# Scores of all pairs in row groups, one tile for the mixing sequences, and two-tensor work on VectorE

## The chip, the cores and the metric

The kernel runs on one core of a Trainium2 chip. The metric is the time of one execution on the device in microseconds (us); lower is better. Engines are named as the profile names them: PE is the matrix engine TensorE (PEld its weight load), DVE is VectorE, ACT is ScalarE, POOL is GpSimd, SP issues most transfers.

## The reference

The reference is a gated linear attention whose output goes through a Fourier mixing layer and a feed-forward network. There are 4 batches, 8 heads, 768 tokens, 48 values a head, so a model width of 384; the hidden width is 1536. All is float32.

```python
for t in range(S):                       # attention, per batch and head
    state = alpha[:, :, t, :, None] * state + einsum('bhd,bhe->bhde', k[:, :, t], v[:, :, t])
    y[:, :, t] = einsum('bhd,bhde->bhe', q[:, :, t], state)
x = y.transpose(0, 2, 1, 3).reshape(B, S, H * D)
X = np.fft.fft(np.fft.fft(x, axis=1), axis=2)      # mixing
u = x + np.real(X)
un = (u - mean(u)) / sqrt(var(u) + 1e-6)           # over the model width
out = u + maximum(un @ w_ch1, 0.0) @ w_ch2
```

## The kernel before, in words

**Pairs.** Two heads make a pair, four pairs a batch, sixteen in all. A pair lies with one head on partitions 0 to 47 and the other on 64 to 111, time along the row. `attn_stages` lists a pair's stages. In `s1` DVE scans alpha forward and backward over 768 steps (tiles `w`, from `w3()`, and `al`), resets at every chunk of 64 and scales every second chunk (`first`). `s2` and `s3` multiply the scanned products into k and q (`times`, tile `kq`). `s4` transposes k (`kt`). `s5` or `s5r` makes the scores of each 128-token block, in two halves of three blocks; ACT moves them out of PSUM and POOL masks them with `affine_select`. `s6` makes the states at block bounds: PE products, then a chain of five DVE operations in `tt`. `s7` multiplies scores and states with v and q; ACT writes the result to two `y` tiles a batch.

**Scores in two forms.** `s5` multiplies the heads apart in plain float32, 64 and 48 partitions deep: the heads lie on different row groups of PE's array. `s5r`, for pairs from number `FR = 7` on, splits q and k into a high and a low part in a faster format (tile `qs`; two ACT activations, one ACT cast and three DVE operations a half) and does both heads in one set of nine matmuls 256 wide a half.

**Mixing.** `combine` takes a pair's columns of the two `y` tiles and forms sum and difference (`sd`, 288 elements a row) and six sequences (`z`, 96 elements each: six two-tensor operations and two with a scalar). The six sequences of a batch lie in three `w3` tiles (`w6`). When the batch is whole, `f2` folds them four ways for the Fourier transform along the width, tile by tile; `mk_s` and `mk_d` are the transforms on PE. Half the tokens come back through memory in reversed order, gathered by POOL's transfers (`f0`). Then `norm_stages` and `ffn_stages`: split operands `x` and `h`, 864 matmuls of 384 columns each way for the run, DVE's `h<-f,h` standing between the two layers.

**Weights.** `wsplit` unpacks twelve tiles of 64-bit words into high and low parts, with three integer operations on DVE, `wm` and `wd` (768 elements, two tensors each) and ACT work. Six are written ahead of the first FFN part, six within it.

**What sets the order.** All operations are recorded first (`Engine.__getattr__`, line 464; nearly every row of the profile has this line). `Plan.emit` then places them one at a time: the engine whose next operation can start earliest, and on it the lowest key among those ready within `WINDOW`. `duration` prices each operation, `LAT` each hop between engines. `FX` names the engines that may do a kind of operation, 'G' being POOL and 'V' DVE; where it names two, the operation goes to one unless the other would be done earlier by `SLACK`. `port` and `held` model that DVE and POOL hinder each other: an overlap lengthens both by half of it. Up to a modelled time of `WARM = 120` us, gaps of PE are filled with small matmuls on `zero` (line 1146). So a changed price or rule reorders all engines.

```python
FX = {'comb': 'G', 'mul': 'VG', 'first': 'G', 'wm': 'VG', 'wd': 'VG', ...}
SLACK = {'ACT': 2.0, 'DVE': 0.5, 'POOL': 5.0}
return [s1, s2, s3, s4, s5 if pair < FR else s5r, s6, s7, lambda: combine(...)]
```

Of the kernel before, what the change touches and what calls it, by code (L numbers as in the profile page):

```python
# [21 lines left out]
DM = H * D  # L22
DFF = 4 * DM
P = 128
# [11 lines left out]
NQS = 3  # L36
FR = 7
# [3 lines left out]
NW3 = 8  # L41
# [133 lines left out]
class Plan:  # L175
# [113 lines left out]
    def duration(self, op, named, engine):  # L289
# [3 lines left out]
        if engine == "PE":  # L293
# [3 lines left out]
            if str(named["1"].real(self.base(named["1"])).dtype).endswith("float32"):  # L297
                slow = 1.65 if self.stride(named["2"]) > 16 else 1.0
                return max(m, slow * n) / 600 + 0.004
# [26 lines left out]
    def port(self, op, named):  # L326

        if op.engine == "POOL":
            return None if "dma" in op.name else "part"
        if op.engine != "DVE" or op.name == "memset":  # L330
            return None
        inputs = [a for k, a in named.items() if k != "out" and isinstance(a, View)]
        wide = [a for a in inputs if a.tile.tag not in ("a", "f1", "f2") and self.region(a)[4] > 1]
        if len(wide) > 1:
            return "part"
        return "whole" if wide and op.name in ("tensor_scalar", "tensor_copy", "copy") and "scalar1" in named else None
# [15 lines left out]
    def emit(self):  # L352
# [13 lines left out]
        held = {"DVE": (0.0, 0.0), "POOL": (0.0, 0.0)}  # L366

        def start(op, e):
# [11 lines left out]
            return t  # L380

        placed = 0
        while placed < len(ops):
            placed += 1
            best = None
            for e, cand in wait.items():
# [4 lines left out]
                for n in cand:  # L391
# [84 lines left out]
SLACK = {'ACT': 2.0, 'DVE': 0.5, 'POOL': 5.0}  # L476
FX = {'comb': 'G', 'mul': 'VG', 'first': 'G', 'wm': 'VG', 'wd': 'VG', 'fold': 'V', 'ev': 'A', 'relu': 'A', 'un': 'V', 'hi': 'A', 'xh': 'A', 'er': 'AV', 'kl': 'V'}
SHARE = 0.5
# [4 lines left out]
def gla_mix_ffn(ctx: ExitStack, tc: tile.TileContext, alpha, kq, v, w1, w2, consts, rowtab, out):  # L483
# [13 lines left out]
        "qs": ([P, 776], F32R, NQS), "sd": ([P, 2, 3, 2 * D], F32, 1), "h": ([P, 776], F32R, 3), "x": ([P, 776], F32R, 6),  # L497
# [151 lines left out]
    def attn_stages(b, hp, i, mixed):  # L649
# [81 lines left out]
        def s5r():  # L731
            e["X"] = []
            for h2 in range(2):
                sl = slice(h2 * DM, (h2 + 1) * DM)
                X = w3()[:, 0:S].rearrange("p (c two n) -> p two c n", two=2, c=3)
                e["X"].append(X)
# [558 lines left out]
```

## Time and profile before

| what | value |
| --- | --- |
| runs shown | 571.16, 571.66, 576.05 us (median 571.66) |
| the profiled execution | 572.74 us, span 570.9 us |
| mean granted clock of TensorE | 0.946 |
| busy: PE, DVE, ACT, POOL | 534.1, 398.2, 195.6, 220.1 us |
| first DFT matmul of the four batches | 83.6, 206.3, 316.0, 427.4 us |
| first FFN matmul | 125.4 us |

A row of a group view names line, engine, operation, `out<-in` with buffer numbers left out, partitions x elements and the count; then busy us and the mean ns of one; then the idle time of the engine ahead of them, and whose end ended it. PE's busy time holds the matmuls on `zero`. A row with three numbers between slashes gives the shortest, median and longest of a group in ns. The chain of waits is the work that ended last, followed back from the end.

### The profile page before, as it was taken

To read this page: it belongs to the slowest core of one execution; us is meant where nothing else is said; L and a number is where in the kernel's file an instruction comes from. 1 tells how busy PE (TensorE), PEld (TensorE's weight loads), DVE (VectorE), ACT (ScalarE), POOL (GpSimd) and SP (SyncE) were. 2 spreads that over 40 slices of the span, in tenths; PEclk is the share of its full clock that TensorE was granted. 3 is DMA by queue.
4 is the path that set the end of the run, shared out by engine and by line. 5 is a ranking of instruction groups with operands and counts; after the bars stand their busy time and mean duration, and the time that the engine had idled before them with its cause. 6 is when DMAs were issued, how large, how long until landed. Compare 5 with 4: busy or idle time off the path is not lost.

```text
span 570.9 us, 10199 instructions
## 1 busy us (share of the span) xinstructions
PE 534.1 (94%) x4018; PEld 510.9 (89%) x4018; DVE 398.2 (70%) x903; ACT 195.6 (34%) x428; POOL 220.1 (39%) x255
## 2 busy tenths in 40 slices
PE   7999879989898999998989999999999999999995
PEld 6888878978887989998979999988999999999995
DVE  7766796898999666999984679989755932412111
ACT  3354422345643522245643213255522121211110
POOL 2557584264758440055857202358770000000000
PEclk8575976999998999999999999999999999999998
DMA  8999080230200250112324300221011100100001
GB/s 223 276 363 270 21 284 15 75 95 1 69 2 2 70 153 1 47 37 78 97 64 142 124 1 1 91 64 29 2 56 29 42 1 0 43 0 27 17 0 48
DMA packets 16550, 42.23 MB, mean 74 GB/s; under 512 B 1904, under 2 KB 7088, under 8 KB 16496
## 3 DMA queue, kind: packets, MB, share of 16 engines
q1 hardware_dynamic: 15440, 39.08, 22.2%
q0 software_dynamic: 768, 2.36, 1.4%
q8 instruction: 34, 0.56, 0.4%
q14 instruction: 20, 0.16, 0.1%
q10 hardware_dynamic: 288, 0.07, 0.1%
HBM read 34.42 MB, written 7.08 MB: 73 GB/s over the span
## 4 chain that ended last, share of the span: by engine, by line
PE 62%; DVE 18%; POOL 7%; DMA 4%; issue 4%; ACT 2%; SPq 1%; POOLq 0%; ACTq 0%; DVEq 0%
PE f L464 42%; PE a L464 19%; DVE w L464 6%; POOL w L464 4%; DMA al<-in_alpha_dram 4%; DVE al L464 3%; POOL sd L464 2%; DVE h L464 2%; PE f L1146 2%; DVE qs L464 2%; DVE x L464 2%; DVE tt L464 1%; DVE y L464 1%; DMA scr<-y 1%; SPq L464 1%
## 5 line engine op out<-in xcount | busy, mean ns | idle before, releaser
L464 PE MATMUL f<-wt,h 128*128 128x384 f32 x864 | 178.4, 342 | 5.1 <-DVE h L464 5.1
L464 PE MATMUL f<-x,wt 128*128 128x384 f32 x864 | 179.0, 343 | 0.8 <-DVE x L464 0.8
L464 PEld LDWEIGHTS f<-wt,h 128*128 128x128 f32 x864 | 149.9, 188 | 7.8 <-DVE h L464 7.2
L464 PEld LDWEIGHTS f<-x,wt 128*128 128x128 f32 x864 | 152.0, 189 | 1.8 <-DVE x L464 1.2
L464 DVE SCALAR_TENSOR_TENSOR h<-f,h 128x384 fp32r<-128x384 f32 x96 | 53.1, 553 | 93.2 <-ACT h L211 92.2
L211 ACT ACTIVATE h<-f 128x384 fp32r<-128x384 f32 x96 | 47.1, 490 | 182.3 <-PE f L464 176.4
L464 POOL TENSOR_SCALAR_AFFINE_SELECT w<-w 128x512 f32<-128x512 f32 (+1 forms) x64 | 47.5, 765 | 44.3 <-ACT w L464 44.3
L464 POOL TENSOR_TENSOR w<-w,rec 112x384 f32<-112x384 f32 (+1 forms) x17 | 18.1, 1065 | 103.3 <-DVE mt L464 45.5
L464 PE MATMUL a<-vn,w 128*128 128x64 f32 x312 | 49.4, 288 | 3.3 <-POOL w L464 2.3
L464 PEld LDWEIGHTS a<-vn,w 128*128 128x128 f32 x312 | 45.1, 208 | 5.3 <-POOL w L464 3.5
L464 POOL TENSOR_TENSOR sd<-y,y 128x288 f32<-128x288 f32 x32 | 33.0, 1052 | 35.6 <-ACT y L464 30.8
L1146 PE MATMUL f<-zero 128*32 128x32 f32 x798 | 36.8, 210 | 3.5 <-ACT w L464 1.9
L464 ACT COPY w<-a 128x512 f32<-128x512 f32 (+6 forms) x58 | 26.2, 481 | 40.2 <-PE a L464 39.0
L1146 PEld LDWEIGHTS f<-zero 128*32 128x32 f32 x798 | 32.8, 125 | 7.6 <-ACT w L464 2.4
L464 DVE TENSOR_TENSOR y<-y,a 128x191 f32<-128x191 f32 (+2 forms) x96 | 28.6, 346 | 13.3 <-PE a L464 13.1
L464 DVE SCALAR_TENSOR_TENSOR tt<-tt,mt 112x96 f32<-112x96 f32 x64 | 35.5, 557 | 0.3
L464 PE MATMUL a<-cst,w 96*128 96x96 f32 (+10 forms) x267 | 34.2, 267 | 1.3 <-DVE w L464 1.2
L464 PEld LDWEIGHTS a<-cst,w 128*96 128x96 f32 (+7 forms) x267 | 32.0, 166 | 3.2 <-DVE w L464 2.2
L464 DVE TENSOR_TENSOR_SCAN al<-al,d 112x768 f32<-112x768 f32 (+1 forms) x17 | 34.6, 2037 | 0.1
L464 PE MATMUL a<-qs,qs 112*128 112x256 f32 x162 | 29.2, 292 | 4.7 <-DVE qs L464 4.7
L464 DVE TENSOR_TENSOR_SCAN w<-al,d 112x768 f32<-112x768 f32 (+1 forms) x17 | 32.3, 1902 | 0.2
L464 PE MATMUL a<-tt,w 112*128 112x96 f32 x134 | 30.4, 312 | 1.1 <-DVE d L464 1.1
(129 smaller groups left out, 737.5 us busy)
## 6 DMA issues: line engine op xcount, KB each, us to landing
kq<-in_kq_dram SPq DMA_DIRECT2D x13, 672.0 KB, 5.4
wt<-in_w_dram SPq DMA_DIRECT2D x8, 768.0 KB, 10.9
al<-in_alpha_dram SPq DMA_DIRECT2D x15, 336.0 KB, 9.7
out_dram<-y SPq DMA_DIRECT2D x24, 192.0 KB, 1.9
vn<-in_v_dram SPq DMA_DIRECT2D x14, 296.0 KB, 3.5
wt<-in_w_dram SPq DMA_DIRECT2D x8, 384.0 KB, 13.0
scr<-y SPq DMA_DIRECT2D x4, 576.0 KB, 3.9
wt<-in_kq_dram SPq DMA_DIRECT2D x2, 672.0 KB, 12.7
```

Source lines behind the costliest of these rows:

```text
L211: return lambda out, x: e.activation(out, x, AF.Relu)
L464: op.ins = op.fns[op.engine](*[real(a) for a in op.args], **{k: real(x) for k, x in op.kwargs.items()})
L1146: plan.idle = (lambda: nc.tensor.matmul(warm[2][0:32, 480:512], zero.real(), zero.real(), start=True, stop=True), 1.0, WARM, ("f2", 2))
```

## The change

`s5r`, its tile `qs` and the bound `FR` go: all sixteen pairs use `s5`. The six sequences of a batch lie in one tile `z`, and a tile `f` takes the fold's intermediate; each step of the fold is one instruction over all six instead of three over two. `f` also serves the normalization of the first half. The pool of `w3` tiles shrinks from 8 to 5.

`comb`, `mul` and `first` may run on DVE alone; `wm` and `wd` keep both engines. In the model, an operation of DVE or POOL that uses the port now waits until the other's is done, instead of both being slowed; `tensor_scalar` with a constant counts as such too. The choice between two engines compares when each would finish, the lock included, and POOL has no slack any more. PE's price of plain float32 matmuls up to 64 partitions deep falls by a fifth.

```diff
-NQS = 3
-FR = 7
-NW3 = 8
+NW3 = 5
...
-                return max(m, slow * n) / 600 + 0.004
+                p0, p1 = self.region(named["1"])[0:2]
+                return max(m, slow * n) / (750 if p1 - p0 <= GRP else 600) + 0.004
...
+        def finish(op, e):
+            t = max(clock[e], start(op, e))
+            return (max(t, held[other[e]]) if op.port and e in held else t) + op.durs[e]
...
-                        done = max(now, t) + op.durs[e] - SLACK[e]
-                        if any(max(clock[o], start(op, o)) + op.durs[o] < done for o in op.engines if o != e):
+                        if any(finish(op, o) < finish(op, e) - SLACK[e] for o in op.engines if o != e):
...
-                other = "POOL" if op.engine == "DVE" else "DVE"
-                a, b = held[other]
-                both = max(0.0, min(b, t + op.dur) - max(a, t))
-                op.dur += (SHARE if op.port == "part" else 1.0) * both
-                if other == "POOL":
-                    clock[other] += SHARE * both
-                held[op.engine] = (t, t + op.dur)
+                op.dur += max(0.0, held[other[op.engine]] - t)
+                held[op.engine] = t + op.dur
...
-SLACK = {'ACT': 2.0, 'DVE': 0.5, 'POOL': 5.0}
-FX = {'comb': 'G', 'mul': 'VG', 'first': 'G', 'wm': 'VG', 'wd': 'VG', 'fold': 'V', ...}
-SHARE = 0.5
+SLACK = {'ACT': 2.0, 'DVE': 0.5, 'POOL': 0}
+FX = {'comb': 'V', 'mul': 'V', 'first': 'V', 'wm': 'VG', 'wd': 'VG', 'fold': 'V', ...}
...
-        return [s1, s2, s3, s4, s5 if pair < FR else s5r, s6, s7, lambda: combine(*mixed(), hp * 2 * D, 2 * D, FL["comb"])]
+        return [s1, s2, s3, s4, s5, s6, s7, lambda: combine(*mixed(), hp * 2 * D, 2 * D, FL["comb"])]
...
-        z = [x[:, c0 : c0 + w] for x in zt[0]]
+        z = [zt[:, i, c0 : c0 + w] for i in range(6)]
...
-            zp = [t.rearrange("p (i n) -> p i n", i=2) for t in zt[1]]
-            fp = [early()[:, 0:S].rearrange("p (i n) -> p i n", i=2) for _ in range(3)]
-            for z, f in zip(zp, fp):
+            z, f = zt, plan.tile("f")
```

The change shows in the order on each engine. POOL, from the first pairs' work on, before (`sd` and `w<-sd` are the combine of the first pair, `w<-w,rec` is `first`, `w<-kq,w` and `al<-kq,al` are `times`):

```order
L464 TENSOR_TENSOR w_2_3_68<-w_2_3_68,rec 112x6x64
L464 AFFINE_SELECT w_4_5_70<-w_4_5_70 128x384 x2
L464 TENSOR_TENSOR al_41_106<-kq_45_110,al_41_106 112x768
L464 TENSOR_TENSOR w_5_6_71<-w_5_6_71,rec 112x6x64
L464 TENSOR_TENSOR w_5_6_71<-wt_0_65_130,w_5_6_71 112x768
L464 TENSOR_TENSOR sd_13_78<-y_23_88,y_24_89 128x288 x2
L464 TENSOR_TENSOR w_6_7_72<-sd_13_78 128x96
L464 TENSOR_TENSOR w_7_8_73<-sd_13_78 128x96
```

And now, from the first pair to the gather of the first batch:

```order
L462 AFFINE_SELECT w_3_4_69<-w_3_4_69 128x384 x2
L462 AFFINE_SELECT w_4_5_70<-w_4_5_70 128x384 x2
L462 AFFINE_SELECT w_0_82_495<-w_0_82_495 128x384 x2
L462 AFFINE_SELECT w_4_85_509<-w_4_85_509 128x384 x2
L462 AFFINE_SELECT w_0_98_636<-w_0_98_636 128x384 x2
```

Products and combines have left POOL; the selects, the gathers and a few weight operations stay.

DVE around the first FFN operands before (`x<-f,x` is the low half of an operand, `al_131` and `al_136` belong to the pairs two and three places into the second batch):

```order
L464 SCALAR_TENSOR_TENSOR al_131_838<-al_131_838,d_141 112x768
L464 TENSOR_TENSOR d_141<-al_136_849 112x12
L464 TENSOR_TENSOR al_131_838<-kq_160_1098,al_131_838 112x768
L464 MEMSET al_136_849 112x13
L464 MEMSET d_141 112x12
L464 TENSOR_TENSOR x_191_1400<-f_1_189_1394,x_191_1400 128x384
L464 TENSOR_TENSOR x_193_1410<-f_0_182_1350,x_193_1410 128x384
L464 TENSOR_TENSOR x_195_1416<-f_1_192_1406,x_195_1416 128x384
```

And now (`al_65` is the first pair of the second batch):

```order
L462 TENSOR_TENSOR x_146_1215<-f_1_143_1192,x_146_1215 128x384
L462 TENSOR_TENSOR x_148_1220<-f_2_144_1194,x_148_1220 128x384
L462 TENSOR_TENSOR x_150_1232<-f_0_145_1196,x_150_1232 128x384
L462 TENSOR_SCALAR x_156_1259<-wt_0_56_121 128x768
L462 SCALAR_TENSOR_TENSOR al_65_327<-al_65_327,d_137 112x768
L462 SCALAR_TENSOR_TENSOR h_158_1268<-f_0_154_1250,h_158_1268 128x384
```

The scans and products of two pairs have moved behind the first FFN operands, among the evacuations `h`.

PE at the scores of pair 7, before (`a_286` and `a_288` take both heads):

```order
L464 MATMUL a_286_1970<-qs_12_77,qs_284_1960 128x256
L464 MATMUL a_286_1970<-qs_281_1937,qs_284_1960 128x256
L464 MATMUL a_288_1976<-qs_12_77,qs_284_1960 128x256
L464 MATMUL a_288_1976<-qs_281_1937,qs_284_1960 128x256
L464 MATMUL a_286_1970<-qs_12_77,qs_284_1960 128x256 x2
L464 MATMUL a_286_1970<-qs_281_1937,qs_284_1960 128x256
```

And now, with each head's scores in a PSUM tile of its own (`a_281`, `a_283` in the first half, `a_285`, `a_287` in the second):

```order
L462 MATMUL a_281_1998<-w_4_260_1848,al_125_835 128x128
L462 MATMUL a_283_2002<-w_4_260_1848,al_125_835 128x128
L462 MATMUL a_281_1998<-w_4_260_1848,al_125_835 128x128
L462 MATMUL a_283_2002<-w_4_260_1848,al_125_835 128x128
L462 MATMUL a_281_1998<-w_4_260_1848,al_125_835 128x128
L462 MATMUL a_283_2002<-w_4_260_1848,al_125_835 128x128
L462 MATMUL a_285_2011<-w_4_260_1848,al_125_835 128x128 x3
L462 MATMUL f_0_274_1958<-x_150_1232,wt_0_235_1708 128x384
L462 MATMUL a_287_2022<-w_4_260_1848,al_125_835 128x128 x3
```

One half of this pair has its heads alternating, the other has them one after the other with an FFN matmul between.

More of the change, by code (lines that the diff above doesn't have):

```diff
@@ L328, in port @@
         if op.engine == "POOL":
-            return None if "dma" in op.name else "part"
-        if op.engine != "DVE" or op.name == "memset":
-            return None
+            return "dma" not in op.name
+        if op.name == "memset":
+            return False
         inputs = [a for k, a in named.items() if k != "out" and isinstance(a, View)]
@@ L334, in port @@
         if len(wide) > 1:
-            return "part"
-        return "whole" if wide and op.name in ("tensor_scalar", "tensor_copy", "copy") and "scalar1" in named else None
+            return True
+        return len(wide) > 0 and "scalar1" in named and not isinstance(named["scalar1"], View)
     def psum(self, view):
@@ L365, in emit @@
         order = []
-        held = {"DVE": (0.0, 0.0), "POOL": (0.0, 0.0)}
+        held = {"DVE": 0.0, "POOL": 0.0}
+        other = {"DVE": "POOL", "POOL": "DVE"}
         def start(op, e):
@@ L473, in __getattr__ @@
         return lambda *a, **k: self.plan.add(self.names, method, a, k)
-SLACK = {'ACT': 2.0, 'DVE': 0.5, 'POOL': 5.0}
-FX = {'comb': 'G', 'mul': 'VG', 'first': 'G', 'wm': 'VG', 'wd': 'VG', 'fold': 'V', 'ev': 'A', 'relu': 'A', 'un': 'V', 'hi': 'A', 'xh': 'A', 'er': 'AV', 'kl': 'V'}
-SHARE = 0.5
+SLACK = {'ACT': 2.0, 'DVE': 0.5, 'POOL': 0}
+FX = {'comb': 'V', 'mul': 'V', 'first': 'V', 'wm': 'VG', 'wd': 'VG', 'fold': 'V', 'ev': 'A', 'relu': 'A', 'un': 'V', 'hi': 'A', 'xh': 'A', 'er': 'AV', 'kl': 'V'}
 WINDOW = {'PE': 0.0, 'ACT': 0.15, 'DVE': 0.05, 'POOL': 0.5, 'SP': 0.0, 'DMA': 0.0}
@@ L496, in gla_mix_ffn @@
         "w3": ([P, 776], F32, NW3), "kt": ([P, NT - 1, CW], F32, 1),
-        "qs": ([P, 776], F32R, NQS), "sd": ([P, 2, 3, 2 * D], F32, 1), "h": ([P, 776], F32R, 3), "x": ([P, 776], F32R, 6),
+        "z": ([P, 6, DM], F32, 1), "f": ([P, 6, DM], F32, 1), "sd": ([P, 2, 3, 2 * D], F32, 1), "h": ([P, 776], F32R, 3), "x": ([P, 776], F32R, 6),
         "y": ([P, 3, DM], F32, NY), "b8": ([P, S], I8, 1), "c8": ([P, S], I8, 1), "st": ([P, 3, 6], F32, 2), "mv": ([P, 3, 2], F32, 2),
@@ L792, in s7 @@
                 FL["ev"].copy(ytiles[h2][:, :, hp * 2 * D : (hp + 1) * 2 * D].rearrange("p a (h e) -> p a h e", h=2), yo)
-        return [s1, s2, s3, s4, s5 if pair < FR else s5r, s6, s7, lambda: combine(*mixed(), hp * 2 * D, 2 * D, FL["comb"])]
+        return [s1, s2, s3, s4, s5, s6, s7, lambda: combine(*mixed(), hp * 2 * D, 2 * D, FL["comb"])]
     def early():
         return plan.tile("x").bitcast(F32) if state["start"] else w3()
-    def w6(new=None):
-        t = [(new or w3)() for _ in range(3)]
-        return [t[i // 2][:, (i % 2) * DM : (i % 2 + 1) * DM] for i in range(6)], [x[:, 0:S] for x in t]
     def combine(ytiles, zt, c0, w, E=None):
@@ L944, in n1 @@
             if blk == 0:
-                uw = [plan.tile("qs").bitcast(F32) if state["start"] else w3() for _ in range(2)]
-                un = [uw[0][:, 0:DM], uw[0][:, DM:S], uw[1][:, 0:DM]]
+                uw = plan.tile("f")
+                un = [uw[:, m] for m in range(3)]
             else:
@@ L1030, in mixed @@
             if b not in sequence:
-                sequence[b] = ([plan.tile("y") for _ in range(2)], w6())
+                sequence[b] = ([plan.tile("y") for _ in range(2)], plan.tile("z"))
             return sequence[b]
@@ L1221, in general_rest @@
                 SY.dma_start(ytiles[h2][:, a].rearrange("p (g n) -> p g n", g=NP2), yv[h2, :, a])
-        zt = w6()
+        zt = plan.tile("z")
         for g in range(NP2):
```

52 lines of the change are left out of this document (12 added, 40 removed).

## The prediction

> **What bounds the kernel now.** I read the profile's page first: its engine totals, its slices and the shares of the chain of work that ended last. Both come from one profiled execution with a span of 570.9 us.
>
> ```profile
> PE 534.1 (94%) x4018; PEld 510.9 (89%) x4018; DVE 398.2 (70%) x903; ACT 195.6 (34%) x428; POOL 220.1 (39%) x255
> PE   7999879989898999998989999999999999999995
> DVE  7766796898999666999984679989755932412111
> PE 62%; DVE 18%; POOL 7%; DMA 4%; issue 4%; ACT 2%; SPq 1%; POOLq 0%; ACTq 0%; DVEq 0%
> ```
>
> PE is busy nearly everywhere, and the last quarter is PE alone. DVE and POOL matter in the first half; together they hold 25% of the chain. So I cut the span into stages with the view of busy time by window. Its columns are window, length, then busy time and (instructions) of PE, PEld, DVE, ACT, POOL, the granted clock, the DMA share and GB/s. The cuts are the first DFT matmuls of the four batches (83.6, 206.3, 316.0, 427.4) and the first FFN matmul (125.4).
>
> ```profile
> 0.00:83.60 83.60, 72.37 (x833) 66.50 (x834) 61.72 (x141) 33.74 (x72) 48.67 (x64) 0.75 0.79 241
> 83.60:125.40 41.80, 39.17 (x460) 34.24 (x458) 34.20 (x105) 12.86 (x31) 16.77 (x14) 0.85 0.24 71
> 125.40:206.30 80.90, 74.56 (x473) 71.00 (x472) 71.51 (x104) 38.80 (x70) 51.67 (x56) 0.98 0.15 44
> 206.30:316.00 109.70, 102.58 (x706) 98.93 (x705) 90.61 (x212) 43.12 (x103) 50.53 (x62) 1.00 0.24 72
> 316.00:427.40 111.40, 108.45 (x740) 104.79 (x739) 89.80 (x213) 42.60 (x101) 50.82 (x61) 1.00 0.13 41
> 427.40:570.90 143.50, 136.93 (x817) 135.46 (x815) 50.40 (x135) 24.52 (x52) 1.61 (x3) 0.99 0.06 21
> ```
>
> The reader is to see two regimes. From 125.4 us on, PE is busy 74.56 + 102.58 + 108.45 + 136.93 = 422.5 of 445.5 us; only 6.3 + 7.1 + 3.0 + 6.6 = 23.0 us are idle. Whatever the change does to DVE and POOL there can win at most those 23, and the 6.6 of the last stage lie behind no pair work at all. Before 125.4, PE's busy time is misleading, for it is filled with dummy matmuls on `zero`; the date of the first FFN matmul is set by DVE, POOL and loads. So the kernel's end is: start of the FFN, plus the PE work left from there, plus PE's idle time from there. I cost the change in these three terms.
>
> **The first term: when the FFN starts.** Two pieces of the chain of waits, and four rows of DVE's timeline (start, length, what, and in brackets the wait ahead):
>
> ```profile
> 63.40 3.20 POOL sd L464 x2
> 66.61 3.28 POOL w L464 x7
> 72.47 3.73 POOL sd L464 x2
> 76.20 2.49 POOL w L464 x3
> 118.52 3.85 DMA al<-in_alpha_dram
> 80.66 1.48 DVE L464 TENSOR_TENSOR x<-w 128x382 f32<-128x382 f32 x3
> 125.01 1.49 DVE L464 TENSOR_TENSOR x<-f,x 128x384 fp32r<-128x384 f32 x3 [0.43 <-ACT x L464]
> 126.42 3.47 DVE L464 TENSOR_SCALAR x<-wt 128x768 int32<-128x768 int32 x1
> 129.97 0.55 DVE L464 TENSOR_SCALAR x<-x 128x768 int32<-128x768 int32 x1
> ```
>
> The two combines that end ahead of the fold take 3.20 + 3.28 + 3.73 + 2.49 = 12.7 us on POOL. The fold starts at 80.66 and the first FFN operand leaves DVE from 125.01: 44.4 us. Within these, DVE does the two scans and the products of two further pairs, and ACT, which must write the high halves first, stands 3.85 us before the check of a late alpha load. The last two rows show why POOL work hurts DVE: the same kind of instruction takes 0.55 us alone and 3.47 beside POOL's combine.
>
> These are the prices of POOL's work and of DVE's (columns: what, shapes, count, busy us, mean ns):
>
> ```profile
> L464 POOL TENSOR_TENSOR sd<-y,y 128x288 f32<-128x288 f32 x32 | 33.0, 1052 | 35.6 <-ACT y L464 30.8 <-DVE x L464 4.8
> L464 POOL TENSOR_TENSOR w<-sd 128x96 f32<-128x96 f32 x64 | 29.4, 480 | 0.0
> L464 POOL TENSOR_TENSOR w<-sd,w 128x96 f32<-128x96 f32 x32 | 17.8, 557 | 0.1
> L464 POOL TENSOR_SCALAR_AFFINE_SELECT w<-w 128x384 f32<-128x384 f32 x28 | 22.5, 824 | 20.6 <-ACT w L464 20.6
> L464 DVE TENSOR_TENSOR w<-w 128x382 f32<-128x382 f32 x18 | 9.6, 560 | 2.5 <-POOL w L464 1.6 <-issue 0.8
> L464 DVE TENSOR_TENSOR w<-w 128x190 f32<-128x190 f32 x18 | 5.6, 348 | 0.0
> L464 DVE TENSOR_TENSOR w<-kq,w 112x768 f32<-112x768 f32 x3 | 3.6, 1213 | 0.0
> L464 DVE TENSOR_TENSOR_SCAN al<-al,d 112x768 f32<-112x768 f32 x15 | 31.6, 2110 | 0.1
> L464 DVE SCALAR_TENSOR_TENSOR qs<-w,hm,qs 112x384 fp32r<-112x384 f32 x36 | 25.4, 729 | 8.0 <-ACT qs L464 8.0
> L464 DVE TENSOR_TENSOR qs<-al,qs 112x384 fp32r<-112x384 f32 x18 | 13.6, 757 | 0.1
> L464 DVE SCALAR_TENSOR_TENSOR tt<-tt,mt x64: 286/320/2234, 18.3 to 417.9; 112x96 f32<-112x96 f32 x64
> L464 DVE SCALAR_TENSOR_TENSOR tt<-tt,mt 112x96 f32<-112x96 f32 x64 | 35.5, 557 | 0.3
> ```
>
> On DVE a two-tensor operation costs, from 348 ns at 190 elements and 560 at 382, about 1.10 ns an element and 0.14 us fixed: 0.46 us for 288 and 0.25 for 96. A combine (two of 288, six of 96) is thus 2 × 0.46 + 6 × 0.25 = 2.4 us on DVE, against (33.0 + 29.4 + 17.8)/16 = 5.0 on POOL. Two of them save 12.7 − 4.8 = 7.9 us of the chain ahead of the fold. Against that stand the products that DVE now does itself, some 1.2 us each, for the four first pairs; DVE has 83.6 − 61.7 = 21.9 us idle in that stage, so most of them find room. I put the fold at 70, between 66 (all saved, and the shorter waits of DVE too) and 78 (nearly all eaten).
>
> From fold to FFN: the order of DVE has only one pair's first scan ahead of the first FFN operand, where it had three pairs' scans. Two pairs less are four scans of about 2.1 us and products of 1.2, some 9 to 11 us, of which about half found idle time: 5. ACT's checks of the two later alphas also come behind the FFN operands now, which takes the 3.85 us away; DVE's norm is next there, so I count 3 of them. The fold in larger pieces saves 48 wide instructions a run at between 0.05 and 0.14 us, a quarter of it here: 1. That makes 44.4 − 9 = 35 us, bounded by 30 and 42. The FFN starts at 70 + 35 = 105; I take 104, since the waits beside POOL shrink here as well.
>
> [...]
>
> **The second term: PE work after that start.** By matmul forms, and by four pieces of PE's timeline:
>
> ```profile
> L464 PE MATMUL a<-vn,w 128*128 128x64 f32 x312 | 49.4, 288 | 3.3 <-POOL w L464 2.3 <-issue 1.0
> L464 PE MATMUL a<-tt,w 112*128 112x96 f32 x134 | 30.4, 312 | 1.1 <-DVE d L464 1.1
> L464 PE MATMUL a<-vn,kt 128*112 128x96 f32 x120 | 15.7, 274 | 0.0
> L464 PE MATMUL a<-cst,al 112*128 112x112 f32 x63 | 10.8, 274 | 1.4 <-DVE al L464 1.4
> 98.52 0.71 PE L464 MATMUL a<-w,al 64*128 64x128 f32 x6
> 99.16 1.13 PE L464 MATMUL f<-cst,x 96*128 96x96 f32 x8
> 105.67 1.16 PE L464 MATMUL f<-w,al 64*128 64x128 f32 x8
> 106.75 0.41 PE L464 MATMUL a<-cst,al 112*128 112x112 f32 x2
> 299.80 1.31 PE L464 MATMUL a<-qs,qs 112*128 112x256 f32 x9
> ```
>
> *Scores.* Half a pair in split form, nine matmuls, takes at most 1.31 us, about 1.15 to the next start; 18 halves are removed: 20.7 us. Half a pair in row groups is 12 records. With the heads alternating they lie on each other: 98.52 to 99.16, 0.64 us. With one head after the other, 8 records took 105.67 to 106.75, 0.135 each, so 12 take 1.6, and 1.8 with a change of form around each. In PE's new order about half of the 18 halves alternate: 9 × 0.64 + 9 × 1.8 = 22.0. Net +1 us, between −9 (all alternate) and +12 (none). The mask's two selects a half stay; 36 activations and 18 casts leave ACT, which costs and wins nothing, as ACT is busy 34%.
>
> [...]
>
> *Work that moves.* By the first FFN matmul the order has had six pairs' scores and five pairs' outputs before, and four and four after. So 10 transposes (0.171 us each, 10.8/63), 10 state products (20 records of 0.131), 24 score matmuls (about 3), 12 output products (24 records of 0.158) and 5 products with `tt` (10 records of 0.227) come later: 1.7 + 2.6 + 3 + 3.8 + 2.3 = 13.4, about 14 us with the switches. The work after the start is then 422.5 + 14 + 1 = 437.5.
>
> **The third term: PE idle after the start.** On DVE the change adds 16 × 2.4 = 38 us of combines, 16 products at 1.2 = 19, 15 of `first` (384 elements, 0.56) = 8 and seven weight operations at up to 1.2 = 8: 73 us. It takes 25.4 + 13.6 = 39 of splitting and 3 to 7 of folding. The rest is relief from POOL: the `tt` row alone has 64 × (557 − 320) = 15 us above its median; the scans, products and splits show the same kind of excess (729 and 757 ns for 384 elements that the rate above prices at 0.56: 54 × 0.18 = 10, but those go anyway). Relief is between 15 and 60; I take 45, since POOL keeps little more than its selects, 64 of some 0.8 us, of its 220 busy us. DVE then stands at 398 + 73 − 39 − 5 − 45 = 382, between 367 and 412. In the first FFN stage, though, it inherits the scans of two pairs from ahead of the start. There I raise PE's idle time from 6.3 to 9; in the next two I lower it from 7.1 to 4 and from 3.0 to 2; the tail keeps 6.6. Together 21.6.
>
> **The sum.** 104 + 437.5 + 21.6 = 563.1 us of span. The profiled execution took 572.74 with its 570.9 of span, and the median of the runs is 571.66, 0.8 above the span. So 563.9, or 564 in a run like those shown: 1.3% less.
>
> **The rivals.**
>
> *DVE becomes the bound (slower).* The place is DVE's queue from the FFN's start to the last batch's fold: combines and products now stand in it ahead of `h<-f,h`, and two hidden matmul groups later PE waits. For it: DVE is busy 71.5 of 80.9, 90.6 of 109.7 and 89.8 of 111.4 us there. Against it: an engine that waits beside POOL counts as busy. It decides if the relief is near its lower end: DVE at 412 is 30 more than in the forecast, some 8 a batch, and busy over nine tenths between folds; 6 us more PE idle in each of three stages give 564 + 18 = 582. Chance 0.20.
>
> *Scores run one head after the other.* Nearly all halves at 1.8 us, or interrupted by FFN matmuls and dearer for it: +11 against split scores instead of +1, so 574; with the FFN starting a little earlier than I say, 569 to 574, no change that shows. Chance 0.20.
>
> *All of it works.* The fold comes at 66, the FFN 30 us behind it at 96 (−8), scores nearly as if alternating (−5), idle 19 (−3): 548. Chance 0.14.
>
> *It does not do what it says.* If the FFN's start is set by the loads (DMA share 0.79 in the first stage), the fold stays near 78 and the start at 115 or later; with 11 us more on the forecast the time is 575, and less than that if fewer operations move. I count it within the chances of the first two rivals, as they give the same times.
>
> **How the numbers follow.** The forecast, 557 to 569, has the remaining 0.46. One per cent (565.9 and 577.4) is about what a measurement of this kernel tells from no change. Faster: 0.36 of the forecast and the 0.14 of the third rival, 0.50. Same: 0.10 of the forecast, 0.18 of the serial scores, 0.02 of a weak DVE bound, 0.30. Slower: 0.18 and 0.02, 0.20. The range from 550 to 579 leaves out the best of the third rival and most of the DVE bound, 0.2 in all.
>
> **What would show it.** In the new profile: the first FFN matmul at 98 to 111 us; `tt` with a mean near 0.35 us; POOL busy under 75 us; DVE busy 367 to 412; half pairs of scores at 0.6 to 0.7 us where the heads alternate and 1.6 to 1.8 where not; PE idle from the FFN's start near 22. The forecast is wrong if the FFN starts after 115, if PE's idle time behind it is above 35, or if the scores on PE cost 8 us more than the split ones.

## The result

The changed kernel takes 569.76 us in the median of 21 executions (565.12 to 579.10), the kernel before 571.66 us in 21 beside them. The ratio is 0.9935 with a 95% interval of 0.9913 to 0.9957: 0.65% faster, where 1.3% was forecast. The sign was right; the size was half, and the result lies in the band that the prediction called the same. Executions scatter with TensorE's granted clock (of the changed kernel, 565.12 us at 0.946 and 576.85 at 0.918), some running a few per cent longer: medians and ranges here are of all executions, ratios leave the long ones out. The profiled execution of the changed kernel took 575.95 us, 6.2 above its median, with a lower clock than most (0.925 against 0.938 in the median one). No execution of this kernel near its median was profiled, so where such an execution may differ is read below from other versions with the same order of work.

The page of the changed kernel, with the rows that answer to those shown of before:

```profile
PE 545.4 (95%) x4150; PEld 523.3 (91%) x4150; DVE 370.4 (65%) x949; ACT 170.7 (30%) x373; POOL 67.5 (12%) x84
PE   7889979769899999999999999999999999999995
DVE  7754798787469969998876995377567612412111
POOL 0120233010101323001123000022220000000000
PEclk8755999687689999999999999999999999999998
PE 82%; DMA 7%; DVE 6%; ACT 2%; issue 1%; SPq 1%; ACTq 0%; DVEq 0%
```

POOL is nearly empty, DVE is 28 us less busy, and DVE and POOL have gone from 25% of the chain of waits to 6%. What is new is the row of the clock: from the eighth slice to the twelfth (100 to 172 us) it stands at 6, 8, 7, 6, 8. The row of the kernel before, which the prediction left out, is at 9 there, with one dip behind, in the thirteenth:

```profile
PEclk8575976999998999999999999999999999999998
```

The same stages as in the prediction, of the changed kernel, cut at the first DFT matmuls (84.9, 223.9, 315.5, 427.0) and the first FFN matmul (113.0), with the same columns:

```profile
0.00:84.90 84.90, 74.17 (x914) 67.96 (x914) 57.39 (x158) 32.11 (x67) 15.01 (x23) 0.76 0.78 228
84.90:113.00 28.10, 23.82 (x328) 20.74 (x328) 22.79 (x76) 8.80 (x17) 5.64 (x3) 0.81 0.15 50
113.00:223.90 110.90, 104.05 (x630) 99.31 (x630) 86.96 (x181) 43.58 (x88) 19.39 (x21) 0.86 0.19 57
223.90:315.50 91.60, 91.37 (x667) 87.80 (x666) 76.91 (x208) 30.30 (x74) 12.30 (x19) 1.00 0.27 83
315.50:427.00 111.50, 111.26 (x780) 107.95 (x779) 78.71 (x211) 30.69 (x76) 14.85 (x21) 1.00 0.14 42
427.00:574.20 147.20, 140.69 (x839) 139.56 (x837) 47.66 (x120) 25.19 (x53) 0.29 (x1) 0.98 0.06 19
```

In the second and third batch PE is idle 0.2 us each, where it was idle 7.1 and 3.0. But the first FFN stage has PE busy for 104 us at a clock of 0.86. The difference of the two profiled executions, in the three terms of the prediction and one that it did not have (work is busy time times clock, loss is busy time times what the clock lacks, for the stages from the FFN's start; the dip of the last slice lies behind the last matmul and is left out):

| term | before | after | difference | forecast |
| --- | --- | --- | --- | --- |
| start of the FFN | 125.4 | 113.0 | −12.4 | −21.4 |
| PE work from there, at full clock | 421.0 | 432.8 | +11.8 | +15 |
| PE idle from there | 23.0 | 13.8 | −9.2 | −1.4 |
| lost to the clock from there | 1.5 | 14.6 | +13.1 | none |
| span | 570.9 | 574.2 | +3.3 | −7.8 |

The clock term alone is larger than the gain that was forecast. It is not a matter of this one execution: the two other profiles of the changed kernel show the same stage at a clock of 0.85, and the two benches below, which begin with the kernel before, lose 1.7 us behind the FFN's start, in one half-clock stretch of 3.4 us each. The loss begins in short stretches in which PE has little to do. Two of them with what follows:

```profile
122.60:126.00 3.40, 1.85 (x17) 1.37 (x13) 3.40 (x8) 0.62 (x2) 0.00 (x0) 1.00 0.00 0
126.00:136.30 10.30, 8.42 (x32) 8.20 (x33) 7.15 (x13) 5.07 (x12) 3.04 (x4) 0.50 0.37 100
143.10:146.50 3.40, 1.10 (x12) 0.95 (x14) 3.40 (x11) 0.69 (x2) 0.00 (x0) 1.00 0.00 0
146.50:163.60 17.10, 17.10 (x78) 16.14 (x75) 7.06 (x18) 5.45 (x11) 2.21 (x4) 0.50 0.28 80
```

For 3.4 us PE is busy 1.85 us in the first and 1.10 us in the second, while DVE is busy without a break: it does the moved products and combines and the weights. In the next stretch the clock is at half, for 10.3 and for 17.1 us, though PE is then busy for 8.4 of 10.3 and for all of 17.1. In the profiles of both kernels the stretches between two changes of the clock last whole multiples of 3.41 us: the longer ones at half in the changed kernel 11, 3, 3 and 5 of them (20.2 to 57.8, 105.6 to 115.8, 126.0 to 136.3 and 146.5 to 163.6 us), the one behind the FFN's start of the kernel before one (181.4 to 184.8). The expectations of the benches call such a length a window. The planner's dummy matmuls, which fill such gaps ahead of the FFN, end with it: they write into a bank in which an FFN accumulator is open, and `emit` leaves them out while it is.

So the theory is: the change does free DVE and start the FFN earlier, and the granted clock takes back what that gives, because the work that moved behind the FFN's start makes thin stretches there. I call it the clock theory. The rivals: the row-group scores or the moved work simply cost PE more (the work theory); or the parts need each other and DVE is the bound.

### The profile page after: what moved, and what is told of

It reads as the page before. It is cut to its first block, busy times and chain, and to the rows that moved or that the text cites. A ratio compares the mean times of both kernels' runs of the same rounds, so it can differ in the third digit from the quotient of the medians.

```text
span 574.2 us, 10199 instructions
## 1 busy us (share of the span) xinstructions
PE 545.4 (95%) x4150; PEld 523.3 (91%) x4150; DVE 370.4 (65%) x949; ACT 170.7 (30%) x373; POOL 67.5 (12%) x84
## 4 chain that ended last, share of the span: by engine, by line
PE 82%; DMA 7%; DVE 6%; ACT 2%; issue 1%; SPq 1%; ACTq 0%; DVEq 0%
PE f L462 57%; PE a L462 23%; DMA al<-in_alpha_dram 3%; DMA w<-in_alpha_dram 3%; PE f L1108 2%; DMA kq<-in_kq_dram 2%; DVE y L462 1%; DVE x L462 1%; DVE w L462 1%; SPq L462 1%; DVE al L462 1%; ACT c L462 1%; DVE st L462 1%; ACT w L462 0%; ACT x L462 0%
## 5 line engine op out<-in xcount | busy, mean ns | idle before, releaser
L462 POOL TENSOR_SCALAR_AFFINE_SELECT w<-w 128x384 f32<-128x384 f32 x64 | 41.4, 667 | 280.7 <-ACT w L462 261.9
L1108 PE MATMUL f<-zero 128*32 128x32 f32 x876 | 42.4, 215 | 4.4 <-ACT w L462 2.8
L462 ACT COPY w<-a 128x384 f32<-128x384 f32 (+4 forms) x58 | 26.4, 481 | 32.6 <-PE a L462 32.4
L462 PE MATMUL a<-w,al 48*128 48x128 f32 (+1 forms) x276 | 32.0, 295 | 4.1 <-ACT w L462 1.9
L462 PEld LDWEIGHTS a<-w,al 48*128 48x128 f32 (+1 forms) x276 | 26.6, 194 | 8.8 <-ACT w L462 2.9
L462 DVE TENSOR_TENSOR sd<-y,y 128x288 f32<-128x288 f32 x32 | 14.0, 477 | 30.9 <-ACT y L462 30.9
L462 DVE TENSOR_TENSOR_SCAN al<-al,d 112x768 f32<-112x768 f32 (+1 forms) x17 | 28.9, 1697 | 0.0
L462 PEld LDWEIGHTS a<-tt,w 112*128 112x128 f32 x134 | 23.7, 215 | 1.5 <-DVE tt L462 0.5
L462 ACT COPY y<-a 128x288 f32<-128x288 f32 x27 | 10.8, 400 | 42.6 <-PE a L462 42.6
L462 DVE TENSOR_TENSOR y<-y,f 128x384 f32<-128x384 f32 (+2 forms) x44 | 21.2, 515 | 3.0 <-PE f L462 2.6
```

The costliest lines, as they stand in the source:

```text
L462: op.ins = op.fns[op.engine](*[real(a) for a in op.args], **{k: real(x) for k, x in op.kwargs.items()})
L1108: plan.idle = (lambda: nc.tensor.matmul(warm[2][0:32, 480:512], zero.real(), zero.real(), start=True, stop=True), 1.0, WARM, ("f2", 2))
```

## The experiments

**Is it the clock?** The changed kernel once more, and again later beside other versions:

> The changed kernel once more, for a profile in which TensorE's clock is as in its faster executions. Clock theory (the first FFN stage, from the first FFN matmul to the second batch's first DFT matmul, loses PE time at half clock): the granted clock of that stage is between 0.86 and 0.97, the stage is shorter than 110.9 us by about half of the half-clock time that is gone, and all later stages keep their lengths within 1 us. Work theory (row-group scores and moved work cost more on PE): the stage keeps a length near 110 us at any clock, and the stages behind it are what differs.

> The changed kernel beside the three that follow, on the same chip: 565 to 571 as in its earlier executions, with the time of an execution rising with its half-clock time (565 at a mean clock of 0.947, 576 at 0.92). If the clock theory is wrong, time and clock vary apart.

The medians are 567.75 (ratio to before 0.9888, interval 0.9829 to 0.9947) and 569.25 (0.9952, 0.9910 to 0.9994). Both profiles fell into executions far above those medians (578.69 and 576.83 us), so they do not show the stage with a better clock, and the first expectation stays untested by them. The second was met: over its ten executions the time falls as the mean clock rises, from 576.83 us at 0.918 to 566.58 at 0.941, and so it does over the 21 first ones.

Then dummy matmuls in the FFN stage, dense:

```diff
+WARM2 = 200.0
-            if op.engine == "PE" and self.idle and t < self.idle[2] and not self.open:
-                for _ in range(int((t - max(clock["PE"], self.idle[1])) / DUMMY)):
-                    order.append(self.idle[0])
+            if op.engine == "PE" and self.idle and t < WARM2 and not (self.open and self.shut):
+                each = DUMMY if t < 60.0 else 0.065
+                for _ in range(int((t - max(clock["PE"], self.idle[1])) / each)):
+                    order.append(self.late[0] if self.open else self.idle[0])
...
+    plan.late = (lambda: nc.tensor.matmul(warm1[1][0:32, 480:512], zero.real(), zero.real(), start=True, stop=True), ("f1", 1))
```

> The changed kernel with the dummy matmuls on zero continued into the first FFN stage (up to 200 us of modelled time instead of 120, also while the FFN's accumulators are open, into another PSUM bank) and placed 1.7 times as densely from 60 us on. Clock theory: no half-clock stretch of over 4 us between 105 and 175 us, first FFN stage 92 to 100 us instead of 111, time 555 to 563. Work theory: the half-clock stretches cost nothing on the path; the dummies only delay PE, time 568 to 576.

> The same more and longer dummy matmuls in the kernel before. Clock theory: before has 3.4 us at half clock behind its FFN start, worth 1.7 us, and some 17 us between 60 and 125 us; time 566 to 573, so that the gap to the changed kernel with the same dummies is 6 us or more. Work theory: as before, 571 to 574.

The changed kernel with them: 566.81 us, 0.9914 (0.9873 to 0.9954), short of 555 to 563. Its first FFN stage:

```profile
107.50:217.20 109.70, 109.61 (x997) 104.13 (x994) 87.21 (x181) 43.36 (x88) 19.14 (x21) 0.95 0.20 58
```

The loss to the clock is 109.61 × 0.05 = 5.5 instead of 14.6 us and the idle time is gone, but 367 more records on PE (997 against 630; a plain float32 matmul makes two, as the 1920 of the first bench below make 3840) fill the stage to nearly the same length, not to the 92 to 100 us expected. So clock and gaps can be bought back, at their price: this many dummies cost what they save. The kernel before with the same rule took 575.66 us in the median of four executions that lie between 568.67 and 579.69, with no interval beside it. By the medians the two are 8.9 us apart, more than the 6 expected, but with that scatter these four do not say whether the kernel before gains.

Dummies made denser only ahead of the FFN (the edit against the dense version):

```diff
-            if op.engine == "PE" and self.idle and t < WARM2 and not (self.open and self.shut):
+            if op.engine == "PE" and self.idle and t < WARM and not self.open:
```

> The changed kernel with dummy matmuls 1.7 times as dense from 60 us of modelled time on, but none behind the FFN's start. Clock theory: the half-clock stretch near 105 to 116 us and part of that before goes, the FFN starts at 107 to 109 instead of 113, and the half-clock stretches near 126 and 146 stay: 562 to 567. Rival (the clock before the FFN's start is of no use, the norm and the loads set it): 567 to 571.

The profile does what the clock theory expects: the FFN starts at 105.8, and the half-clock stretches behind it stay. It is an execution of 567.89 us and shows the first FFN stage at the same loss as above, 104.89 × 0.14 = 14.7 us:

```profile
0.00:105.80 105.80, 94.37 (x1553) 86.75 (x1553) 80.44 (x233) 40.75 (x83) 22.35 (x25) 0.92 0.66 197
105.80:217.10 111.30, 104.89 (x648) 100.22 (x644) 87.05 (x181) 43.62 (x88) 18.77 (x21) 0.86 0.19 59
```

The median, though, is 570.39 (0.9976, 0.9933 to 1.0020): no gain, and in the range of the rival. Whether an earlier FFN pays this run does not say, for 105.8 may be no earlier than usual: versions with the changed kernel's own order up to the FFN start it at 105.1 to 106.4 in three of four profiles (see the first term below).

Last, few of the added dummies and only behind the FFN's start, 83 of them:

```diff
+            if op.engine == "PE" and self.idle and t < (WARM2 if self.open else WARM) and not (self.open and self.shut):
+                each = 0.13 if self.open else DUMMY
```

> The changed kernel with 83 more dummy matmuls (5.4 us at full clock) placed in modelled gaps behind the FFN's start alone, half as many there as in the run with dense ones. Clock theory: the clock loss of the first FFN stage falls from 14 us to under 7 and the dummies fit mostly into the 7.3 us that PE was idle there; the stage takes 100 to 106 us instead of 111, time 560 to 566. Rival (the gate falls for other reasons than thin windows, or dummies cost what they save): stage 109 to 113, time 567 to 572.

> The changed kernel with the thin dummies again: 556 to 561. If its time was a lucky draw of the clock, 564 to 570.

558.27 us in five executions, 0.9730 (0.9645 to 0.9815), and 563.65 in four, 0.9796 (0.9714 to 0.9878). The second median lies between the two expectations; its four executions reach from 557.65 to 565.62. Both intervals lie below that of the changed kernel's 21 executions: 83 matmuls that compute nothing make it 1.4 to 2% faster. With the dummies left out, the order on PE, DVE, ACT and POOL is that of the changed kernel record by record, so the gain is not one of order. The second run's stages, in an execution of 565.62 us, are to be set beside those of the changed kernel:

```profile
0.00:113.10 113.10, 101.45 (x1241) 91.65 (x1241) 80.19 (x233) 40.79 (x83) 21.60 (x25) 0.74 0.61 184
113.10:214.70 101.60, 99.90 (x797) 94.47 (x796) 87.31 (x181) 43.47 (x88) 18.60 (x21) 0.98 0.22 64
214.70:306.00 91.30, 91.30 (x667) 87.89 (x666) 76.59 (x208) 29.86 (x74) 11.41 (x18) 1.00 0.27 81
306.00:417.50 111.50, 111.26 (x780) 107.95 (x779) 78.73 (x211) 30.86 (x76) 14.82 (x21) 1.00 0.13 42
```

The FFN starts at the same 113 us, and the first FFN stage is 9.3 us shorter, 101.6 against 110.9, with the clock at 0.98 instead of 0.86. The later stages are at most 0.8 us shorter, so 9.3 of the 10.3 us between these two executions come from that stage. The first run's profile, of 565.05 us, shows less:

```profile
106.40:213.60 107.20, 105.80 (x796) 100.44 (x796) 87.34 (x181) 43.36 (x88) 19.10 (x21) 0.93 0.20 59
142.80:156.40 13.60, 13.60 (x55) 13.16 (x54) 5.72 (x12) 4.89 (x10) 0.52 (x1) 0.50 0.51 150
```

Here one half-clock stretch is left, the loss is 105.80 × 0.07 = 7.4 us, just above the 7 expected, and the stage takes 107.2, between the 100 to 106 of the clock theory and the 109 to 113 of its rival. The same kernel thus keeps the clock in one execution and loses part of it in another, and why stays open. In both the loss is smaller than without the dummies, which compute nothing and move nothing. That shows the clock theory for the first FFN stage, and this version beats both kernels.

**Do the scores cost?** The kernel before with row-group scores for all pairs (`FR = 16`), and the changed kernel with the two heads tied to alternate, alone and with the thin dummies:

```diff
-FR = 7
+FR = 16
```

> The kernel before with the row-group scores for all sixteen pairs and nothing else (FR = 16). By the prediction's price PE gets 1 us more and DVE loses 39 us, of which the third and fourth stage can give back at most their idle 7.1 and 3.0 us: 563 to 572. Rival (scores run one head after the other): PE gets 8 to 12 us more in stages that are full: 574 to 582.

```diff
+        def follow(*tiles):
+            n, op = len(plan.ops) - 1, plan.ops[-1]
...
+            if e["last"] is None:
+                for t in tiles:
+                    op.slots.append(t)
+                    t.uses += 1
+            else:
+                op.deps.add(e["last"])
+            e["last"] = n
```

> The changed kernel with the two heads' score matmuls tied into alternating order from pair 8 on (a pair of PSUM tiles is taken at once). If serial heads are what the scores cost: PE's score work falls from 36.8 to 26 to 30 us, the third and fourth batch's stages, which PE fills, shorten by 7 to 10 us together, time 557 to 563. If the row-group price is of no weight here, or taking two PSUM tiles at once stalls the pairs: score work falls, PE idle rises as much, 566 to 571.

> Both of the two edits before. If they act in different stages they add: 552 to 560. If the clock edit is worth nothing, as the kernel with alternating heads alone.

Row-group scores in the kernel before: 1.0025 (0.9987 to 1.0063), no gain and no loss that the interval shows, and 579.18 us in the median. The ratio lies between the two expectations, the median in that of the rival. The price on PE was near: matmul by matmul to the next start, times the clock, all scores take about 36.4 us of PE before and 36.8 in the changed kernel. With the heads alternating this falls to 30.6, just above the 26 to 30 expected. Yet the time does not fall: 573.13 us, 0.9919 (0.9839 to 0.9998), an interval that holds the changed kernel's. The first and second stages behind the FFN's start show most of where the 6 us went:

```profile
105.10:219.10 114.00, 106.11 (x626) 101.01 (x625) 86.53 (x181) 43.83 (x88) 16.26 (x20) 0.82 0.18 56
219.10:312.40 93.30, 90.15 (x670) 85.95 (x669) 78.26 (x209) 30.64 (x74) 12.85 (x18) 1.00 0.26 80
```

PE is idle 3.2 us in the second instead of 0.2, and the clock of the first is lower still: 106.11 × 0.18 = 19.1 us lost. Two PSUM tiles must now come free at once, but the waits of that stage end with DVE and POOL tiles, so that this is what stalls PE is not shown. With the thin dummies the loss goes and the kernel takes 559.38 us, 0.9769 (0.9703 to 0.9835). That is inside the 552 to 560 expected of edits that add, but no better than the thin dummies alone, so no gain from alternating heads is seen.

**Which part carries the gain?** The moved work and the lock alone on the kernel before, and the scores, the tile and the fold alone in the changed one, without and with thin dummies:

```diff
-SLACK = {'ACT': 2.0, 'DVE': 0.5, 'POOL': 5.0}
-FX = {'comb': 'G', 'mul': 'VG', 'first': 'G', ...}
+SLACK = {'ACT': 2.0, 'DVE': 0.5, 'POOL': 0}
+FX = {'comb': 'V', 'mul': 'V', 'first': 'V', ...}
```

> The kernel before with the moved work and the lock alone (FX, SLACK, the port model, the price of row groups): split scores from pair 7 on, the sequences in three tiles and the fold by tiles stay. Theory one (the gain is the relief of DVE from POOL; the row-group scores take some of it back, by work left behind and by clock): 560 to 566, with at most 2 us less PE idle than the changed kernel and fewer half-clock windows behind the FFN's start. Theory two (the parts need each other, since the 39 us of splitting now stand on the same DVE as the combines): 568 to 578, with DVE over nine tenths busy in the second and third batch.

> The changed kernel with the old table of engines, slack, port model and price: so row-group scores, one tile and the long fold, with combines and products on POOL. Theory one: the gain is gone, 571 to 580, POOL over 180 us busy, DVE's tt above 0.5 us in the mean. Theory two (the fold and the one tile carry the gain): 562 to 568.

> The moved work and the lock alone (split scores, three tiles, fold by tiles), with thin dummies behind the FFN's start (75). If the relief of DVE and POOL carries the gain: 554 to 562, the clock loss of the first FFN stage under 7 us instead of 14. If the scores and the fold carry a good part: 564 to 570.

> Scores, one tile and long fold alone, combines and products on POOL, with thin dummies behind the FFN's start (44). If the relief carries the gain: 566 to 574. If the scores and the fold carry a good part: 556 to 564.

| version | median us | ratio to before (95%) |
| --- | --- | --- |
| moved work and lock alone | 568.75 | 0.9888 (0.9787 to 0.9989) |
| the same with thin dummies | 564.27 | 0.9800 (0.9721 to 0.9879) |
| scores, tile and fold alone | 571.37 | 0.9929 (0.9871 to 0.9987) |
| the same with thin dummies | 581.52 | 1.0113 (1.0039 to 1.0188) |

The moved work and the lock, by themselves, give as much as the whole change, with and without the dummies. DVE there is 403 us busy with the splitting still on it, and with thin dummies PE is idle 3.8 us in the second batch and 0.0 in the third, so DVE is no bound. The scores, the tile and the fold are not needed for the gain. Without dummies they gave as much alone (0.9929; POOL 195 us busy, `tt` 466 ns), where no gain was expected, so without dummies the parts cannot be told apart. With dummies they can: 0.9800 against 1.0113. The times do not sit well in the ranges: 564.27 us is at the lower edge of what was expected if the scores carry a good part, although this version loses nothing to the clock in its first FFN stage, and 581.52 is above both ranges. Nor does 568.75, which is in the range of the parts that need each other, but without that theory's sign, a DVE over nine tenths busy (0.87 and 0.85 in the second and third batch, with thin dummies). Each half alone loses the clock in the first FFN stage, 104.03 × 0.13 = 13.5 us for the moved work and 86.14 × 0.10 = 8.6 for the other, so the loss does not hang on the row-group scores alone:

```profile
119.30:227.60 108.30, 104.03 (x622) 99.69 (x622) 85.18 (x187) 43.80 (x88) 18.93 (x20) 0.87 0.18 55
113.70:206.50 92.80, 86.14 (x537) 82.34 (x537) 70.91 (x116) 40.82 (x77) 51.10 (x57) 0.90 0.20 60
```

That the scores, the tile and the fold are worth nothing cannot be said, because their slowest version loses its time to the clock too, in another place:

```profile
379.60:383.00 3.40, 2.72 (x16) 2.04 (x14) 2.48 (x7) 1.26 (x5) 3.40 (x8) 1.00 0.01 2
383.40:414.20 30.80, 30.80 (x147) 29.04 (x146) 7.45 (x16) 5.95 (x14) 13.54 (x27) 0.50 0.04 11
```

PE is busy through 30.8 us at half clock, 15.4 us lost, behind a stretch in which PE was busy 2.72 of 3.40 us. This is what the last two runs are about.

**What moves the clock?** Blocks of plain float32 matmuls behind the kernel before, which leave its output alone. Each bench was run once. First, rows:

```python
for kinds, count in (((whole,), 240), ((top,), 320), ((whole,), 240), ((top, low), 320), ((whole,), 240), ((low,), 320), ((whole,), 240)):
    for i in range(count):
        r, t = kinds[i % len(kinds)]
        nc.tensor.matmul(t[:, 384:512], cst.real()[r, 0:128], cst.real()[r, 128:256], start=True, stop=True)
```

> The kernel before, followed by a row of plain float32 matmuls 128x128 that leave the output alone: 240 over all 128 rows, 320 over the top 64 rows, 240 over all, 320 alternating between the top and the bottom 64, 240 over all, 320 over the bottom 64, 240 over all, each block without a gap. Activity theory (the clock gate counts rows at work, not busy time): the clock falls to half within two windows of the blocks over 64 rows and stays there, about 0.43 us a matmul, and is full in the blocks over all rows and in the alternating one, 0.21 us a matmul or, with the groups beside each other, 0.11. Busy theory: PE has no gap, so the clock is full from the second window to the end and a matmul over 64 rows takes 0.21 us.

The blocks over all rows, over the top 64 and alternating between top and bottom:

```profile
564.00:617.00 53.00, 53.00 (x477) 53.00 (x476) 0.62 (x2) 0.00 (x0) 0.00 (x0) 1.00 0.04 13
618.00:689.00 71.00, 71.00 (x638) 71.00 (x637) 0.00 (x0) 0.00 (x0) 0.00 (x0) 1.00 0.00 1
743.00:779.00 36.00, 36.00 (x642) 35.87 (x641) 0.00 (x0) 0.00 (x0) 0.00 (x0) 1.00 0.01 2
```

The clock stays full over 64 rows: 0.111 us a record over all rows (53.00/477) and over 64 (71.00/638), 0.056 alternating. The activity theory's expectation fell; 64 rows alone did not let a full clock fall in 71 us. That alternating heads run beside each other is shown by itself here, a factor of two.

Second, small matmuls, with and without a pause of 14.6 us ahead:

```python
block(128, 120, plain); block(64, 400, plain); block(128, 120, plain)   # columns moved, count
for n in (64, 128):
    ...  # PE waits for 24 copies on VectorE
    block(n, 300, plain)
    block(128, 120, plain)
```

> The kernel before, followed by plain float32 matmuls over all 128 rows that leave the output alone: 120 with 128 columns moved, 400 with 64, 120 with 128; then a pause of PE of over 10 us, 300 with 64 columns and 120 with 128; the same pause, 300 with 128 columns and 120 with 128. If small matmuls keep PE too little at work: the clock falls in the block of 400 or, at least, does not come back in the block of 300 behind the pause, and does in the one of 128 columns within two windows of 3.4 us. If busy time alone counts: the clock holds in the block of 400 and comes back within 7 us behind either pause.

The block of 64 columns without a pause, the one behind the pause, and the block of 128 columns behind that; then PE's timeline from each of the two pauses on:

```profile
590.00:678.00 88.00, 88.00 (x791) 88.00 (x790) 0.00 (x0) 0.00 (x0) 0.00 (x0) 1.00 0.00 1
721.00:848.00 127.00, 127.00 (x597) 127.00 (x596) 0.00 (x0) 0.00 (x0) 0.00 (x0) 0.50 0.00 1
856.00:878.00 22.00, 22.00 (x199) 22.00 (x198) 0.00 (x0) 0.00 (x0) 0.00 (x0) 1.00 0.00 1
720.96 157.54 PE L1152 MATMUL f<-cst 128*128 128x64 f32 x840
893.68 96.32 PE L1152 MATMUL f<-cst 128*128 128x128 f32 x840
```

Small matmuls held a full clock here, but did not bring it back: behind the pause the same instructions run 127 us at half clock with PE busy throughout. At full clock a record of 64 columns takes 0.111 us (88.00/791), as long as one of 128 (22.00/199), so a fully busy PE moves half as many columns with the small ones. The clock returned about 6 us after the 128-column block began, and as fast behind the second pause, which blocks of 128 columns followed directly. Both are estimates. Behind the second pause 840 records in 96.32 us are 3.1 us more than at 0.111 us each, so 6.2 us at half clock. The row of the first holds 600 records of 64 columns, which end near 848.6 at 127.00/597 us each, and 240 of 128, which take the 29.9 us to 878.5: 3.3 us more, so 6.6. So a pause cost little here where these large matmuls followed and much where these small ones did. That is how the 17.1 us of the changed kernel look: they are filled with scores over 64 rows and with products of 64 columns, as in these two rows of PE's timeline there. Scores over 64 rows behind a pause were not tried by themselves.

```profile
147.82 1.01 PE L462 MATMUL f<-vn,w 128*128 128x64 f32 x4
149.24 3.06 PE L462 MATMUL f<-w,al 64*128 64x128 f32 x14
```

## Why the prediction was right or wrong

**The sum itself failed.** "Start of the FFN, plus the PE work left from there, plus PE's idle time from there" holds the clock as it was. Before, the clock lost 1.5 us behind the FFN's start; after, 14.6. The clock row was not weighed, although the prediction itself moved two pairs' small matmuls and DVE work into a stage where no dummies run. With the thin dummies the time is 558 to 564 us, on and below the 564 forecast. That the change without them came within 6 us of the forecast is partly luck: PE's idle time came out 7.8 us and its work 4.7 us below their terms, which pays back most of the clock's 14.6.

**The first term.** 104 was forecast, and the profiled execution shows 113.0, outside the bounds of 98 to 111. The fold was put at 70. Its first instructions, and a window of the changed kernel ahead of it:

```profile
L462 DVE TENSOR_TENSOR f<-z x12: 174/1341/1353, 79.2 to 423.8; 128x1146 f32<-128x1146 f32 x8, 128x12 int32<-128x12 int32 x4
20.20:57.80 37.60, 35.27 (x315) 32.19 (x316) 20.10 (x53) 12.95 (x29) 3.69 (x4) 0.50 0.94 280
```

It starts at 79.2. For 37.6 us ahead of it PE runs at half clock, busy for nearly all of them. But this is not the fold of every execution. Nine profiles have the same order of all engines up to the fold: three of the changed kernel, and one each of the two runs with thin dummies, the two with alternating heads and the two with dense dummies. In four of them (the changed kernel's three and the second thin one) the clock is at half from 37 to 58 us, the fold starts at 79.1 to 79.9 and the FFN at 112.5 to 113.6. In the other five the clock is back at 37 us, the fold starts at 71.0 to 73.0 and the FFN at 105.1 to 107.5. The changed kernel, and the run with alternating heads (an execution of 572.19 us), from 37 to 58 us:

```profile
37.00:58.00 21.00, 20.00 (x183) 18.58 (x181) 12.18 (x35) 6.14 (x16) 3.79 (x5) 0.51 0.87 243
37.00:58.00 21.00, 18.91 (x242) 17.02 (x240) 17.56 (x46) 8.98 (x22) 6.50 (x8) 1.00 1.02 292
```

So the fold at 70 and the FFN at 104 were sized well for executions in which the clock comes back early, and the forecast has no word for the others. The changed kernel's 36 executions lie at 565.1 to 571.0 us (24) and 573.0 to 579.1 (12), about as far apart as the two starts; all three profiles come from the second group. That the first group starts the FFN near 106 is an estimate from the versions with the same order; with the other terms as in the table it gives 106 + 432.8 + 13.8 + 14.6 = 567 us of span, 568 of time. That the clock makes the difference in the start is read from these profiles and was not tried by itself. What comes after the fold was sized well in both: 33 to 35 us to the FFN against 35.

**The second term** held: +11.8 us of work against +15, and the scores +0.4 against +1. One price in it was misread, though: the row of 0.64 us at 98.52 has six records, and half a pair has twelve. Twelve that alternate take 0.86 us to the next start in the run with alternating heads, and six of one head take 0.87 in the changed kernel, so twelve in a row take about the 1.8 that was forecast:

```profile
256.10 0.94 PE L462 MATMUL a<-w,al 64*128 64x128 f32 x12
256.96 0.97 PE L462 MATMUL f<-x,wt 128*128 128x384 f32 x4
259.37 0.93 PE L462 MATMUL a<-w,al 64*128 64x128 f32 x6
260.24 0.62 PE L462 MATMUL f<-wt,h 128*128 128x384 f32 x2
```

So the two orders lie closer than the prediction had it. The 0.2 us in its 1.8 for a change of form, and the 0.6 that its moved work has for switches, are shown by no run: the eight serial records of before come to 1.6 for twelve at 0.135 each, the six here to 1.74 at 0.145. The tail grew by 3.7 us, from 143.5 to 147.2 us, with 140.7 us of PE busy in it instead of 136.9.

**The third term** was too careful. DVE's own prices were right:

```profile
L462 DVE TENSOR_TENSOR sd<-y,y 128x288 f32<-128x288 f32 x32 | 14.0, 477 | 30.9 <-ACT y L462 30.9
L462 DVE TENSOR_TENSOR z<-sd 128x96 f32<-128x96 f32 x64 | 17.2, 289 | 0.0
L462 DVE TENSOR_TENSOR z<-sd,z 128x96 f32<-128x96 f32 x32 | 9.6, 298 | 0.0
L462 DVE SCALAR_TENSOR_TENSOR tt<-tt,mt 112x96 f32<-112x96 f32 x64 | 21.1, 333 | 0.4
```

0.46 and 0.25 us were forecast for the combine, 0.48 and 0.29 came; `tt` fell from 557 ns to 333, near the 350 named. POOL's 67.5 us lie under the 75, DVE's 370 inside 367 to 412 and below the 382 taken. PE's idle time fell to 13.8, not 21.6: the relief was larger than I took, and in the second and third batch PE had almost nothing left to wait for.

**The rivals.** DVE as the bound did not come: it is busy 76.9 of 91.6 and 78.7 of 111.5 us, and PE waits 0.2. Serial scores did not: the halves are partly serial as read from the order, but forcing them apart gave no time. The forecast and its best case were right about DVE and POOL; what no rival had was a PE at a lower clock.

## What to carry to other kernels

A change that takes work off a helper engine can also change when the matrix engine pauses and what follows the pause, as it did here; add a clock term to the sum, stage by stage, from the granted clock's row. In the bench a pause ahead of matmuls of 64 columns was followed by 127 us at half clock, one ahead of 128 columns by about 6 us, so fill such gaps sparingly with dummies. To put large matmuls behind them instead was not tried in a kernel. Where the planner models no clock, look for stages in which its filler is switched off.

## What the runs showed of the hardware

What held the clock did not always bring it back, and PE's busy time alone did not decide it. In one execution, the second bench's, matmuls of 64 moved columns kept it full for 88 us and left it at half for 127 us, with PE busy throughout in both; matmuls of 128 columns brought it back in about 6 us. The 127 us are 37 of the 3.41 us whose multiples its stretches last in the profiles of both kernels. What sets it is not settled: 64 rows out of 128 held the clock full for 71 us.

In these profiles what DVE pays beside POOL goes largely with what POOL does. The mean of `tt` is 271 ns above its shortest 286 of before with POOL busy 220 us, 180 above with 195 (scores, tile and fold alone), 89 above with 63.6 (moved work and lock alone) and 47 above with 67.5 in the changed kernel. The last two show that POOL's busy time is not all of it.
